# A GEGLU feed-forward kernel on one core: x's first tokens loaded in two halves of D, the first weight half tiles over ScalarE, and the products of the first two blocks side by side

## The chip, the core and the metric

The kernel runs on one core of a Trainium2 chip. The core has a matrix engine (TensorE, called PE in the profile, with its weight loads shown apart as PEld), three elementwise engines (VectorE = DVE, ScalarE = ACT, GpSimd = POOL) and SyncE (SP), which here issues nearly all DMAs. Each engine takes its instructions in program order. The engines run beside each other and wait for each other on semaphores. The metric is the device time of one execution in microseconds (us), lower is better.

## What is computed

```python
B, S, D, F = 32, 32, 1024, 3584          # all operands bf16
# x (B,S,D), w_gate (D,F), w_up (D,F), w_down (F,D)
def reference(x, w_gate, w_up, w_down):
    return (_gelu(x @ w_gate) * (x @ w_up)) @ w_down
```

There are 1024 tokens (B times S). Both stages are large matrix products: 1024 x 1024 x 7168 for gate and up, and 1024 x 3584 x 1024 for down.

## The kernel before

**Stage 1** (to about 184 us) computes gate and up for one block of 128 columns of F at a time, 28 blocks in all. It treats each block as a 2 by 2 block product and does it with seven products instead of eight (the Winograd form of Strassen). The rows of the left side are gate and up, and its columns are the two halves of D: `a11`, `a12` are the block's w_gate for the first and second half of D, `a21`, `a22` the same of w_up. The right side is x transposed: `B11`, `B21` hold the first 512 tokens for the first and second half of D, `B12`, `B22` the other 512 tokens. Each product is 4 matmuls of 128 x 128 by 128 x 512 (`KH` = 4 steps of 128 along half of D).

The products by their names in the code, for block i:

- first (P1) a11 x B11 and second (P2) a12 x B21 accumulate in the same PSUM tile `A[i]`, bf16 operands. P1 alone is copied out by ScalarE to `E1`, and after P2 ScalarE writes gelu(A) to `GL`. These two need only w_gate and the first tokens.
- fifth (P5) S1 x T1 into `Y[i]`; sixth (P6) S2 x T2 and seventh (P7) S3 x T3 accumulate in `X[i]`, which ScalarE has seeded with E1 (`seed`). After P6 ScalarE copies X out (`E2`), after P7 again (`e3`), and VectorE adds e3 and Y to `U1`. Fourth (P4) C22 x T4 goes on in X, third (P3) S4 x B22 goes on in Y.
- The sums S1 to S4 are made for each block from the four weight tiles, `C22` is a copy of a22; T1 to T4 are sums of the B tiles and are made once, by VectorE, after all of x has landed (`t_sum`, lines 245 to 248). All of these are fp32 for the PE.

In PSUM four buffers with tag "p" hold the warm-up results and then the X tiles, four with tag "q" hold the A and Y tiles. A new A or Y waits until the tile four places before it has been read.

**Order around the change.** The program order is written by hand. The time before the first data is filled by 18 warm-up matmuls on zeros (`NWARM`, line 136). SyncE issues, in this order: the transposing DMA of the first 512 tokens (1 MB, `xt0`, line 135), the second D half of gate tile 0 (two blocks of columns, 512 KB whole), gate tile 1, the first two blocks of up tile 0, gate tiles 2 and 3, the transposing DMA of the other 512 tokens (`xt1`, line 146), gate tile 4, the rest of up tile 0. The first D half of gate tile 0 is issued by ScalarE, after a small Copy that reads the result of warm-up matmul 3. While x's second half is on its way, PE does P1 and P2 of blocks 0 to 7 (`LEAD` = 8, lines 255 to 262; P2 of block 7 comes later). Then follow P5 of blocks 0 and 1, P1 of block 8 and P2 of block 7 (`ahead()`, line 279), P6 and P7 of blocks 0 and 1 one block after the other, P1 of 9 and P2 of 8, and P4 and P3 of both. VectorE in the same time makes the sums of blocks 0 and 1 (lines 241 to 244), T1 to T4, and the early sums of block 2; GpSimd starts on its sums when its instruction `held` (line 252) has seen the end of T4.

**The loop** (line 296) then goes over blocks 2 to 27. Each pass does P6 and P7 and P5 of block i, P4 and P3 of block i-1, and in most passes P1 and P2 of blocks further on. GpSimd makes most of the sums.

**Stage 2** (line 328 on) does the down projection in the same seven-product form from the tile `gT`. The change does not touch it.

Of the kernel before, what the change touches and what calls it, by code (L numbers as in the profile page):

```python
# [12 lines left out]
def kernel(  # L13
# [18 lines left out]
    nc = tc.nc  # L32
# [16 lines left out]
    assert N == 2 * NB and DT % 2 == 0 and D % DB == 0 and FT % 4 == 0  # L49
    NWARM = 18  # L50
    LEAD = 8
# [29 lines left out]
    def load_gate(c, queue, lo=0, hi=DT):  # L81
        if c not in WG:
            WG[c] = gw.tile([P, DT, 2 * P], bf16, name="gw", tag="gw")
        queue.dma_start(
            out=WG[c][:, lo:hi, :], in_=wg_r[:, lo:hi, 2 * c * P : (2 * c + 2) * P]
        )
# [12 lines left out]
    def a11(i):  # L99
        return block(WG, 2, i, 0)  # L100

    def a12(i):
        return block(WG, 2, i, 1)
# [21 lines left out]
    def psum_q(name):  # L125
        return psum.tile([P, NB], fp32, name=name, tag="q")

    with tc.manual_schedule():
# [5 lines left out]

        nc.sync.dma_start_transpose(out=xt0, in_=xf[0:NB, :])
        for n in range(NWARM):
            nc.tensor.matmul(warm[n % 4], lhsT=zt[:, 0:P], rhs=zt, start=True, stop=True)
            if n == 3:
                nc.scalar.activation(table, warm[n][:, 0:8], ACT.Copy)
                load_gate(0, nc.scalar, 0, KH)  # L140
        load_gate(0, nc.sync, KH, DT)
        load_gate(1, nc.sync)
        load_up(0, 0, 2)
        load_gate(2, nc.sync)
        load_gate(3, nc.sync)
# [35 lines left out]

        def first_product(i):
            A[i] = psum_q("a")
            product(A[i], a11(i), B11)
            if i % 2 == 0:
                E1[i // 2] = ring.tile([P, 2, NB], fp32, name="e1", tag="ring")
            nc.scalar.activation(E1[i // 2][:, i % 2, :], A[i], ACT.Copy)  # L187

        def second_product(i):
            product(A[i], a12(i), B21, first=False)  # L190
            if i % 2 == 0:
                GL[i // 2] = half.tile([P, 2, NB], bf16, name="gl0", tag="half")
            nc.scalar.activation(GL[i // 2][:, i % 2, :], A[i], ACT.Gelu_apprx_tanh)

# [5 lines left out]

        done = 0

        def ahead():
            nonlocal done
            if done < FT:
                first_product(done)
            if done:
                second_product(done - 1)
            done += 1

        def sixth_product(i):
            product(X[i], S2[i], T["T2"], first=False)
            E2[i] = epool.tile([P, NB], fp32, name="e2", tag="e2")
            nc.scalar.activation(E2[i], X[i], ACT.Copy)  # L214

# [7 lines left out]

        def seventh_product(i):
            product(X[i], S3[i], T["T3"], first=False)
            e3 = epool.tile([P, NB], fp32, name="e3", tag="e3")
            nc.scalar.activation(e3, X[i], ACT.Copy)  # L227
            U1[i] = epool.tile([P, NB], bf16, name="u1", tag="u1")
            nc.vector.tensor_tensor(U1[i], Y[i], e3, ALU.add)  # L229

# [38 lines left out]
        for k in range(KH):  # L269
            for i in range(2):  # L270
                nc.tensor.matmul(  # L271
                    Y[i],
                    lhsT=S1[i][:, k, :],
                    rhs=T["T1"][:, k, :],
                    start=(k == 0),
                    stop=(k == KH - 1),
                    skip_group_check=True,
                )
# [12 lines left out]
        copy_a22(2)  # L291
        finish(0)
# [3 lines left out]
        for i in range(2, FT + 1):  # L296
            here, prev, more = i < FT, i - 1 if i > 2 else None, i + 1 < FT
            if more:
                early_sums(i + 1)
            if here:  # L300
                sixth_product(i)
                if more:
                    seed(i + 1)
# [11 lines left out]
            if here:  # L315
                seventh_product(i)
                if more:
                    copy_a22(i + 1)
# [197 lines left out]
```

## Time and profile before

| | |
|---|---|
| time, median of 3 runs | 277.59 us (277.51 to 277.72) |
| the profiled execution's own time | 277.56 us |
| its span in the profile | 275.8 us (1.76 us lie outside) |
| PE busy | 270.0 us, 98% of the span |
| PEld / DVE / ACT / POOL busy | 190.5 / 189.2 / 138.1 / 88.6 us |
| moved by DMA | 26.42 MB, mean 96 GB/s |
| granted TensorE clock | 9 tenths or more in all 40 slices |

The page of the profile lists busy times, the span in 40 slices, DMA queues, the chain of work that ended last, groups of instructions, and DMA issues. In a line of a timeline the first number is the start in us from the span's start, the second how long it took in us, then engine, source line, operation, output and input by their names in the program, how many there are (x), and in brackets how long the engine sat idle before and what released it. "SPq" and "ACTq" are DMAs issued by SyncE and ScalarE; their data moves in the DMA queues q1 and q10. In a list of DMA issues the last number is the median time in us from issue to landing.

### The profile page before, as it was taken

What the parts mean: (1) busy time and instruction counts of PE and PEld (TensorE: products, weight loads), DVE (VectorE), ACT (ScalarE), POOL (GpSimd) and SP (SyncE); (2) the same over time, 40 slices, a digit from 0 to 9 for tenths busy, and PEclk for the clock granted to TensorE, in tenths of its full rate; (3) what the DMA queues carried; (4) which work ended last, traced back from release to release, by engine and by line L of the source; (5) the groups of instructions that cost most, each with busy time, mean ns of one, the idle gap of its engine ahead of it and who ended that gap; (6) DMA issues with size and microseconds to landing.
All of it is one profiled execution on the core that took longest, in us unless ns stands there. A gap on an engine that the chain in (4) does not pass through costs nothing.

```text
span 275.8 us, 3328 instructions
## 1 busy us (share of the span) xinstructions
PE 270.0 (98%) x1179; PEld 190.5 (69%) x1194; DVE 189.2 (69%) x227; ACT 138.1 (50%) x237; POOL 88.6 (32%) x81
## 2 busy tenths in 40 slices
PE   8999999999999999999999999999999999999995
PEld 3446767777677776777766777764447888888883
DVE  0279865667666676666766555759994999999900
ACT  2488475665656665666656666532100082870311
POOL 0000484458554585545854444600000000000000
PEclk9999999999999999999999999999999999999999
DMA  8996420522062071152420120259702000000221
GB/s 194 286 280 157 150 71 5 156 77 76 18 212 76 0 225 37 46 154 76 154 76 9 67 58 22 88 188 324 239 0 76 2 0 0 0 2 0 96 96 38
DMA packets 40912, 26.42 MB, mean 96 GB/s; under 512 B 9152, under 2 KB 40896, under 8 KB 40896
## 3 DMA queue, kind: packets, MB, share of 16 engines
q1 hardware_dynamic: 40224, 25.82, 32.0%
q10 hardware_dynamic: 672, 0.39, 0.5%
q8 instruction: 9, 0.15, 0.2%
q14 instruction: 7, 0.06, 0.1%
HBM read 22.02 MB, written 2.10 MB: 87 GB/s over the span
## 4 chain that ended last, share of the span: by engine, by line
PE 96%; DMA 3%; issue 0%; ACT 0%
PE x L113 28%; PE x L371 18%; PE y L113 18%; PE a L113 17%; PE y L371 9%; PE z L371 4%; DMA xt<-in_x_dram 3%; PE y L271 1%; ACT o_sb L483 0%
## 5 line engine op out<-in xcount | busy, mean ns | idle before, releaser
L113 PE MATMUL x<-T,s 128*128 128x512 f32 x224 | 63.5, 408 | 0.0
L113 PE MATMUL a<-xt,gw 128*128 128x512 bf16 x212 | 51.0, 380 | 1.1 <-DMA xt<-in_x_dram 0.4
L175 POOL TENSOR_TENSOR s<-gw,s 128x512 fp32r<-128x512 bf16 x26 | 30.4, 1171 | 62.4 <-PE y L113 61.7
L113 PEld LDWEIGHTS x<-T,s 128*128 128x128 f32 x224 | 41.7, 188 | 10.8 <-ACT e L214 0.4
L229 DVE TENSOR_TENSOR u<-y,e 128x512 bf16<-128x512 f32 x28 | 19.2, 690 | 34.8 <-ACT e L227 34.1
L171 DVE TENSOR_TENSOR s<-s,gw 128x512 fp32r<-128x512 f32 x28 | 40.8, 1457 | 0.0
L113 PEld LDWEIGHTS <-gw 128*128 128x128 bf16 x224 | 20.2, 98 | 27.6 <-issue 5.7
L218 DVE TENSOR_TENSOR gT<-gl,x 128x512 bf16<-128x512 bf16 x28 | 19.1, 686 | 18.4 <-PE x L113 18.4
L236 ACT ACTIVATE gl<-h 128x512 bf16<-128x512 bf16 x28 | 17.7, 631 | 27.4 <-DVE h L234 27.4
L113 PE MATMUL x<-T,c 128*128 128x512 f32 x112 | 30.2, 393 | 0.0
L113 PE MATMUL y<-B,s 128*128 128x512 f32 x112 | 30.0, 391 | 0.0
L167 POOL TENSOR_TENSOR s<-gw,uw 128x512 fp32r<-128x512 bf16 x25 | 29.2, 1168 | 0.0
L166 POOL TENSOR_TENSOR s<-uw 128x512 fp32r<-128x512 bf16 x25 | 29.1, 1164 | 0.0
L187 ACT ACTIVATE e<-a 128x512 f32<-128x512 f32 x28 | 16.7, 597 | 22.9 <-PE a L113 22.8
L113 PE MATMUL y<-T,s 128*128 128x512 f32 x104 | 27.8, 389 | 0.0
L371 PE MATMUL x<-tc,sc 128*128 128x512 f32 x112 | 25.7, 389 | 0.0
L113 PEld LDWEIGHTS y<-B,s 128*128 128x128 f32 x112 | 21.0, 188 | 4.8
L113 PEld LDWEIGHTS x<-T,c 128*128 128x128 f32 x112 | 20.9, 188 | 4.8 <-ACT e L227 0.5
L371 PEld LDWEIGHTS x<-tc,sc 128*128 128x128 f32 x112 | 21.0, 188 | 4.4
L227 ACT ACTIVATE e<-x 128x512 f32<-128x512 f32 x28 | 16.8, 599 | 14.4 <-PE x L113 14.4
L113 PEld LDWEIGHTS y<-T,s 128*128 128x128 f32 x104 | 19.5, 188 | 4.1
L371 PEld LDWEIGHTS <-gT 128*128 128x128 bf16 x112 | 10.9, 98 | 13.2 <-issue 0.3
(52 smaller groups left out, 325.0 us busy)
## 6 DMA issues: line engine op xcount, KB each, us to landing
gw<-in_w_gate_dram SPq DMA_DIRECT2D x13, 512.0 KB, 3.9
uw<-in_w_up_dram SPq DMA_DIRECT2D x6, 1024.0 KB, 6.4
v<-in_w_down_dram SPq DMA_DIRECT2D x5, 512.0 KB, 3.8
v<-in_w_down_dram SPq DMA_DIRECT2D x4, 640.0 KB, 7.9
v<-in_w_down_dram SPq DMA_DIRECT2D x8, 256.0 KB, 4.3
out_dram<-o_sb SPq DMA_DIRECT2D x15, 128.0 KB, 1.7
uw<-in_w_up_dram SPq DMA_DIRECT2D x2, 512.0 KB, 6.0
gw<-in_w_gate_dram ACTq DMA_DIRECT2D x1, 256.0 KB, 4.4
```

Of the source, the lines that this page charges most:

```text
L113: nc.tensor.matmul(ps, lhsT=lhs[:, k, :], rhs=rhs[:, k, :], start=(first and k == 0), stop=(k == KH - 1), skip_group_check=True,)
L166: engine.tensor_tensor(S1[i], a21(i), a22(i), ALU.add)
L167: engine.tensor_tensor(S3[i], a11(i), a21(i), ALU.subtract)
L171: nc.vector.tensor_tensor(S2[i], S1[i], a11(i), ALU.subtract)
L175: engine.tensor_tensor(S4[i], a12(i), S2[i], ALU.subtract)
L187: nc.scalar.activation(E1[i // 2][:, i % 2, :], A[i], ACT.Copy)
L218: nc.vector.tensor_tensor(gT[:, i, 0:NB], GL[i // 2][:, i % 2, :], X[i], ALU.mult)
L227: nc.scalar.activation(e3, X[i], ACT.Copy)
L229: nc.vector.tensor_tensor(U1[i], Y[i], e3, ALU.add)
L236: nc.scalar.activation(G1[i], h1, ACT.Gelu_apprx_tanh)
L271: nc.tensor.matmul(Y[i], lhsT=S1[i][:, k, :], rhs=T["T1"][:, k, :], start=(k == 0), stop=(k == KH - 1), skip_group_check=True,)
L371: nc.tensor.matmul(ps, lhsT=lhs[:, i, t * P : (t + 1) * P], rhs=rhs[:, i, :], start=(first and j == 0 and i == 0), stop=(last and j == JF ...
```

## The change

The transposing load of the first 512 tokens is cut in two: `B11` (first half of D) is loaded first. ScalarE then issues the first half of gate tile 0 after warm-up matmul 1 instead of 3, and writes 8 columns into `B21`; because of that write SyncE's load of `B21`, which overwrites them, waits for ScalarE. ScalarE also issues the second half of gate tile 0, after warm-up matmul 8 (before, SyncE issued it). Gate tile 1 comes in two DMAs, and the first blocks of up tile 0 come behind gate tile 2 instead of before it. There are 11 warm-up matmuls instead of 18.

In the stretch of the first blocks, P2 of block 7 is done before P5 of blocks 0 and 1, and the work on ScalarE between the blocks is reordered. P6 of blocks 0 and 1 are done side by side (two steps of one block, two of the other, and so on), and so are P7. P1 of blocks 8 and 9 lie between P5, P6 and P7, and P2 of block 8 behind P7. P4 and P3 go block by block. VectorE makes the early sums of block 2 after the `U1` of both blocks instead of before, `held` now reads S2 of block 2, and GpSimd makes S1 and S3 of block 3 before S4 of block 2. From block 3 on the loop is as before.

```diff
-    NWARM = 18
+    NWARM = 11
...
-        nc.sync.dma_start_transpose(out=xt0, in_=xf[0:NB, :])
+        nc.sync.dma_start_transpose(out=B11, in_=xf[0:NB, 0 : KH * P])
         for n in range(NWARM):
             nc.tensor.matmul(warm[n % 4], lhsT=zt[:, 0:P], rhs=zt, start=True, stop=True)
-            if n == 3:
-                nc.scalar.activation(table, warm[n][:, 0:8], ACT.Copy)
-                load_gate(0, nc.scalar, 0, KH)
-        load_gate(0, nc.sync, KH, DT)
-        load_gate(1, nc.sync)
+            if n in (1, 8):
+                nc.scalar.activation(table, warm[n % 4][:, 0:8], ACT.Copy)
+                load_gate(0, nc.scalar, *((0, KH) if n == 1 else (KH, DT)))
+            if n == 1:
+                nc.scalar.activation(B21[:, 0, 0:8], table, ACT.Copy)
+        nc.sync.dma_start_transpose(out=B21, in_=xf[0:NB, KH * P : D])
+        load_gate(1, nc.sync, 0, KH)
+        load_gate(1, nc.sync, KH, DT)
+        load_gate(2, nc.sync)
         load_up(0, 0, 2)
-        load_gate(2, nc.sync)
         load_gate(3, nc.sync)
         nc.sync.dma_start_transpose(out=xt1, in_=xf[NB:N, :])
         load_gate(4, nc.sync)
...
+        def pair_product(ps, lhs, rhs, first, cuts):
+            for lo, hi in zip(cuts, cuts[1:]):
+                for p, l in zip(ps, lhs):
+                    for k in range(lo, hi):
+                        nc.tensor.matmul(
+                            p,
+                            lhsT=l[:, k, :],
+                            rhs=rhs[:, k, :],
+                            start=(first and k == 0),
+                            stop=(k == KH - 1),
+                            skip_group_check=True,
+                        )
...
+        def sixth_products(*blocks):
+            cuts = range(0, KH + 1, 2)
+            pair_product([X[i] for i in blocks], [S2[i] for i in blocks], T["T2"], False, cuts)
+            for i in blocks:
+                E2[i] = epool.tile([P, NB], fp32, name="e2", tag="e2")
+                nc.scalar.activation(E2[i], X[i], ACT.Copy)
...
-        early_sums(2, nc.vector)
-        second_sum(2)
-        held = spool.tile([P, 8], f32r, name="held", tag="held", bufs=1)
-        nc.gpsimd.tensor_copy(held, T["T4"][:, KH - 1, 0:8])
-
-        between = {2: lambda: copy_a22(0), 4: lambda: seed(0), 6: lambda: seed(1)}
+        between = {2: lambda: seed(0), 4: lambda: seed(1), 6: lambda: copy_a22(0)}
         for n in range(0, LEAD, 2):
-            first_product(n)
-            first_product(n + 1)
+            first_products(n)
+            first_products(n + 1)
             if n in between:
                 between[n]()
-            second_product(n)
-            if n + 2 < LEAD:
-                second_product(n + 1)
-        done = LEAD
+            second_products(n)
+            second_products(n + 1)
...
-        ahead()
-        sixth_product(0)
-        sixth_product(1)
-        seventh_product(0)
-        seventh_product(1)
-        ahead()
+        first_products(8)
+        sixth_products(0, 1)
+        first_products(9)
+        seventh_products(0, 1)
+        second_products(8)
+        early_sums(2, nc.vector)
+        second_sum(2)
         seed(2)
-        fourth_product(0)
-        fourth_product(1)
-        third_product(0)
-        third_product(1)
+        held = spool.tile([P, 8], f32r, name="held", tag="held", bufs=1)
+        nc.gpsimd.tensor_copy(held, S2[2][:, KH - 1, 0:8])
+        early_sums(3)
         late_sums(2)
+        for i in range(2):
+            fourth_product(i)
+            third_product(i)
         copy_a22(2)
         finish(0)
...
         for i in range(2, FT + 1):
             here, prev, more = i < FT, i - 1 if i > 2 else None, i + 1 < FT
-            if more:
+            if more and i > 2:
                 early_sums(i + 1)
             if here:
-                sixth_product(i)
+                sixth_products(i)
```

`seventh_products` is cut the same way as `sixth_products`; `first_products` and `second_products` are the old functions for one or more blocks.

More of the change, by code (lines that the diff above doesn't have):

```diff
@@ L180, with first_products, second_products @@
         A, E1, GL = {}, {}, {}
[L182 to L193, printed above, removed]
+        def pair_product(ps, lhs, rhs, first, cuts):
[10 more added lines that the diff above has]
+                        )
+        def first_products(*blocks, cuts=(0, KH)):
+            for i in blocks:
+                A[i] = psum_q("a")
+            pair_product([A[i] for i in blocks], [a11(i) for i in blocks], B11, True, cuts)
+            for i in blocks:
+                if i % 2 == 0:
+                    E1[i // 2] = ring.tile([P, 2, NB], fp32, name="e1", tag="ring")
+                nc.scalar.activation(E1[i // 2][:, i % 2, :], A[i], ACT.Copy)
+        def second_products(*blocks, cuts=(0, KH)):
+            pair_product([A[i] for i in blocks], [a12(i) for i in blocks], B21, False, cuts)
+            for i in blocks:
+                if i % 2 == 0:
+                    GL[i // 2] = half.tile([P, 2, NB], bf16, name="gl0", tag="half")
+                nc.scalar.activation(GL[i // 2][:, i % 2, :], A[i], ACT.Gelu_apprx_tanh)
         X, Y, E2, U1, G1 = {}, {}, {}, {}, {}
@@ L199, in seed @@
             nc.scalar.activation(X[i], E1[i // 2][:, i % 2, :], ACT.Copy)
-        done = 0
+        done = LEAD + 2
         def ahead():
@@ L205, in ahead @@
             if done < FT:
-                first_product(done)
-            if done:
-                second_product(done - 1)
+                first_products(done)
+            second_products(done - 1)
             done += 1
[L211 to L214, printed above, removed]
+        def sixth_products(*blocks):
+            cuts = range(0, KH + 1, 2)
+            pair_product([X[i] for i in blocks], [S2[i] for i in blocks], T["T2"], False, cuts)
+            for i in blocks:
+                E2[i] = epool.tile([P, NB], fp32, name="e2", tag="e2")
+                nc.scalar.activation(E2[i], X[i], ACT.Copy)
         def fourth_product(i):
@@ L222, in fifth_product, with seventh_products @@
             product(Y[i], S1[i], T["T1"])
[L224 to L229, printed above, removed]
+        def seventh_products(*blocks):
+            cuts = range(0, KH + 1, 2)
+            pair_product([X[i] for i in blocks], [S3[i] for i in blocks], T["T3"], False, cuts)
+            for i in blocks:
+                e3 = epool.tile([P, NB], fp32, name="e3", tag="e3")
+                nc.scalar.activation(e3, X[i], ACT.Copy)
+                U1[i] = epool.tile([P, NB], bf16, name="u1", tag="u1")
+                nc.vector.tensor_tensor(U1[i], Y[i], e3, ALU.add)
         def third_product(i):
@@ L268 @@
             Y[i] = psum_q("y")
[L269 to L278, printed above, removed]
-        ahead()
-        sixth_product(0)
-        sixth_product(1)
-        seventh_product(0)
-        seventh_product(1)
-        ahead()
+        pair_product(
+            [Y[0], Y[1]], [S1[0], S1[1]], T["T1"], True, range(KH + 1)
+        )
+        first_products(8)
[5 more added lines that the diff above has]
+        second_sum(2)
         seed(2)
-        fourth_product(0)
-        fourth_product(1)
-        third_product(0)
-        third_product(1)
+        held = spool.tile([P, 8], f32r, name="held", tag="held", bufs=1)
+        nc.gpsimd.tensor_copy(held, S2[2][:, KH - 1, 0:8])
+        early_sums(3)
         late_sums(2)
+        for i in range(2):
+            fourth_product(i)
+            third_product(i)
         copy_a22(2)
@@ L315 @@
             if here:
-                seventh_product(i)
+                seventh_products(i)
                 if more:
```

## The prediction

> **What bounds the kernel now.** I read the chain that ended last first, because it tells whether any engine but PE matters; then its pieces in order of time, to find what is not PE; then the timeline of the first 35 us and the DMA queues in short windows, since the change lies there.
>
> ```profile
> PE 96%; DMA 3%; issue 0%; ACT 0%
> ...
> 0.73 7.18 DMA xt<-in_x_dram
> 7.91 0.04 issue
> 7.96 6.85 PE a L113 x31
> 14.81 0.05 issue
> 14.86 6.21 PE a L113 x28
> 21.07 1.85 PE y L271 x8
> 22.91 1.74 PE a L113 x8
> 24.65 3.75 PE x L113 x16
> ```
>
> The chain is 7.96 us of waiting for the first tokens and then PE without a break to 272.4 us. The change leaves PE's matmuls as they are, 7 warm-ups apart, so it can win time only by starting the row of products earlier, and lose it only by breaking the row. A matmul costs 13.11/60 = 0.2185 us here (7.96 to 21.07, 60 matmuls by the code). P1 of blocks 0 and 1 are 8 of them, 1.75 us, so P2 of block 0, the first to need the second half of D, starts at 9.71. That instant is the yardstick: behind it both kernels have the same PE work, and if no new gap opens the end moves as it moves.
>
> ```profile
> 1.19 6.33 PE L137 MATMUL warm<-zt 128*128 128x512 bf16 x18 [1.19 <-DVE zt L130]
> 3.17 0.18 ACT L139 ACTIVATE table<-warm 128x8 bf16<-128x8 f32 x1 [0.94 <-PE warm L137]
> 3.19 0.43 ACTq L84 DMA_DIRECT2D gw<-in_w_gate_dram  x1
> 4.59 1.11 SPq L84 DMA_DIRECT2D gw<-in_w_gate_dram  x2
> 7.67 0.10 PEld L113 LDWEIGHTS <-gw 128*128 128x128 bf16 x1 [0.65 <-DMA gw<-in_w_gate_dram]
> 19.26 2.50 DVE L157 TENSOR_TENSOR T<-xt,xt 128x512 fp32r<-128x512 bf16 x4 [1.86 <-DMA xt<-in_x_dram]
> 26.22 2.35 DVE L157 TENSOR_TENSOR T<-xt,T 128x1024 fp32r<-128x1024 bf16 x2
> 34.32 0.69 DVE L234 TENSOR_TENSOR h<-y,e 128x512 bf16<-128x512 f32 x1 [0.70 <-ACT gl L236]
> ```
>
> See here that the first weights come hardly before x (7.67 against 7.96), and that VectorE stands still until 19.26 for x's other tokens and is then busy to 34. The queues, in the windows 5.5 to 6 and 6 to 6.5 us:
>
> ```profile
> q1 hardware_dynamic: 523, 0.13, 117.7%
> q10 hardware_dynamic: 27, 0.01, 9.6%
> ...
> q10 hardware_dynamic: 290, 0.15, 106.5%
> q1 hardware_dynamic: 52, 0.01, 11.7%
> ```
>
> ScalarE's queue (q10) moved nothing before about 5.85, though its load was issued at 3.19: it waited until the transposing load on SyncE's queue (q1) was nearly through. Then it ran almost alone for 0.9 us. q1's next load began only at 6.7, though issued at 4.59. Summed in steps of 0.2 us, the transposing load moves from 2.1 to 6.15, has 2048 of its 4096 packets done at 4.2, and is seen landed at 7.91, 1.76 us behind its last data. A weight half tile is seen 0.7 us after its last data.
>
> **The change, part by part.** The sum is made against the profiled execution, 277.56 us, 0.03 under the median of the runs; I count these as equal.
>
> *First half of x alone.* B11 is half the packets: data to 4.2, seen between 4.65 (the other transposing load was seen about 0.45 behind its last data, 18.7 against 19.13) and 5.96 (1.76 behind). I take 5.96, the row of the same place.
>
> *Gate half tile over ScalarE.* Warm-up 1 ends two slow matmuls in; these stand 0.427 apart. 3.17 - 2 x 0.427 = 2.31, the issue at 2.33, its data behind B11 from 4.2 to 5.1, seen at 5.8. The warm-ups cost 11 x 0.427 and end at 5.9: the weight loads step at 0.43 until 5.43 and at 0.22 from 5.85, so what is dropped is the 7 fast ones. P1 thus starts near 6.0 and is through at 7.75.
>
> *The held half.* ScalarE's Copy into B21 comes after its DMA issue (0.43), at 2.76, and ends at 2.95; SyncE issues B21 at 3.0 instead of as part of the first load. The whole load's issue held SyncE 3.79 us, so a half 1.9, to 4.9. Behind it in SyncE's queue stand all weight loads and xt1. First data comes 1.3 to 1.4 us after an issue (0.73 to 2.1), so at 4.4, when the gate half tile still fills the engines: no hole. B11, B21 and the half tile have the same bytes as xt0 and the half tile before, whose data ended at 6.95. So B21's data ends at 6.95 and is seen between 7.4 (+0.45) and 8.7 (+1.76). I take 8.7: as before, another queue's load runs beside its end.
>
> *The second gate half tile.* Its issue waits for warm-up 8: 1.19 + 9 x 0.427 + 0.27 (the release in the line at 3.17) = 5.3, against 4.59 on SyncE before. Its landing is what the trace of before does not show. Lower bound: it does what ScalarE's load did before, starts at 6.6 or as B21's data ends, runs almost alone while q1 stands between two loads, and is seen at 6.95 + 0.9 + 0.7 = 8.55. Middle: it shares the engines with gate tile 1, issued by SyncE at 4.9 and 5.4; both half tiles end at 8.75, seen at 9.45. Upper bound: it waits behind the whole of gate tile 1, as long as that took from issue to landing (5.2), so 10.5. I take 8.7, nearest to the only row in which the two queues met behind a transposing load.
>
> The Trainium skill, "DMA: Bandwidth & Descriptors", section "Issuing engines are not separate DMA queues", says that DMAs of all issuing engines interleave on the same 16 engines, so another queue saves only issue time. By that rule the half tile shares with gate tile 1 and lands at 9.45. This trace disagrees for the first load (q10 idle from its issue to 5.85, then alone), so I hold the rule for the second case, not the first.
>
> So P2 of block 0 starts at 8.8 (B21 or gate, 8.7, and 0.05 to 0.1 to start) and not at 9.71: **0.9 us earlier**. PE stands from 7.75 to 8.8, so it does not matter whether P1 begins at 6.0 or 7.0.
>
> *What is late next.* up tile 0's first blocks come behind gate tile 2, 512 KB later at 290 GB/s: at 13.97, where gate tile 2 landed before, not at 12.24. VectorE's 8 sums (12.25 to 17.40, 5.15 us) then end at 19.1. Their cover is the wait for xt1 to 19.26: 0.14 us are left, cost 0. xt1 itself has the same bytes ahead of it. GpSimd has nothing yet.
>
> *P5 and the pairs.* All 64 matmuls of blocks 0 to 7 now end at 8.8 + 56 x 0.2185 = 21.05, so P5 starts when it did before, and the last piece of T1, ready at 21.75, is needed at 22.4. P1 of block 8 to 23.8, P6 from there (T2 whole at 24.03, its second half needed at 24.7), P1 of 9 to 26.5, P7 to 28.3 (T3 at 26.3; E2 of block 1 at 26.4, needed at 26.95), P2 of 8 to 29.2. P4 of block 0 needs T4 (28.57). Cost 0 to -0.1: the row of 16 matmuls took 3.75 us where the f32 rows of 4 at 0.91 give 3.64. I take 0.
>
> *VectorE after T4.* U1 of both blocks, 1.28, then three sums of block 2, 1.81, then gT, h1, gT, h1 at 0.64 to 0.69: 28.49 + 1.28 (or 29.9, by e3 of block 1) + 1.81 + 2.7 = 34.3 to 34.4 for the last h1. It frees the PSUM of block 1's Y, which P1 of block 10 needs; PE is there at 35.62 - 0.9 = 34.7. Slack 0.3; cost 0, and every us by which xt1 is later costs the rest. With no slack used, this wait caps the gain at about 1.3.
>
> *GpSimd's order.* `held` waits for S2 of block 2, at 31.7, and took 1.79; S1 of block 3 at 34.7, VectorE's S2 of block 3 by 36.4 (it took 1.64 beside GpSimd), needed by P6 of block 3 at 37.1. S4 of block 2 at 37.1 is needed near 43. Cost 0; its cover is the 0.7 us. ScalarE's cost in the blocks, about 3.0 of each 3.5 us, is unchanged.
>
> Sum: 277.56 - 0.9 = **276.66, say 276.7 us**.
>
> **The rivals.**
>
> *A tie by sharing.* The second half tile shares with gate tile 1 and is seen at 9.45; P2 starts at 9.5, gain 0.2, 277.35 (277.05 to 278.1 with small losses). For it: its issue is 0.7 us later than before, and gate tile 1 is ahead of it. It also covers the change not doing what it says: B11 no earlier than x's whole now (7.91) puts P2 at 9.66, no gain. Against it: q10's row above.
>
> *Slower by the late gate half.* The half tile's descriptors wait behind all of gate tile 1, as ScalarE's first load waited 2.66 us for its first packet. Then it is seen at 10.5, P2 starts at 10.55: +0.85, 278.4. It decides from 10.27 on (9.71 + 0.56). For it: a load of 256 KB took 4.4 us from ScalarE, and 5.32 + 5.2 = 10.5 is what the tile ahead takes. Against it: what held the first load was a transposing load of 1 MB; gate tile 1 is half that.
>
> *Slower by a slow PE.* The matmul rate doubled at 5.85, after 11 slow warm-ups, and now the warm-ups end right there, with a stand of 1 us soon behind. If PE is slow again from 8.8 for 16 matmuls, that is 16 x 0.21 = 3.35 us: 280.0; for 8, 278.3. Against it: the trace has 0.43 us idle at 7.5 with no slow matmul behind it, nothing longer. The Trainium skill, "TensorE: Matmul & The Clock Gate", Part 1, says that PE is slowed after an idle window of some 3.4 us, which a stand of 1 us is not; no run here shows it.
>
> *The gain eaten by VectorE.* xt1 0.5 us later takes 0.2 of the gain: 276.9; 1 us later 277.4. SyncE's split loads speak for it, the unchanged bytes against it.
>
> **How the numbers follow.** Under 0.2% of 277.59, 0.56 us, no measurement of this kernel tells a change from none: the bounds are 277.03 and 278.15. My forecast holds 0.50, with its own range 276.2 (gain 1.36, the cap and the small gap) to 277.0. The tie holds 0.23, VectorE 0.09 (two thirds of it still faster), the late gate half 0.12, the slow PE 0.06. Faster 0.50 + 0.06 = 0.56; same 0.23 + 0.03 = 0.26; slower 0.18. The range for 8 in 10 goes from 276.1 (0.1 below the cap, which is itself a sum of rows) through the tie to 278.4, the late gate half.
>
> **What would show it.** P1 starting near 6.0, and a stand of PE near 7.75 to 8.8 on DMA gw or DMA xt: how it ends decides between forecast, tie and late half. q10's packets between 6.6 and 8.8 show whether its load ran alone. x's other tokens at 19.3, PE without a break after 8.8, and no matmul of P1 at 0.43 apart show the rest. I am wrong if PE stands past 9.7, if T1 starts past 19.8, or if PE waits for VectorE near 34.

## The result and the profile after

The changed kernel takes 278.2 us (median of 10 runs, 277.81 to 278.43) against 277.56 us (277.45 to 277.72, 10 runs): a ratio of 1.0021, 95% interval 1.0012 to 1.0029. It is slower by 0.21%, where I had forecast 276.7 and a gain of 0.9 us. The profiled execution took 278.29 us with a span of 276.5.

The chain that ended last, of the changed kernel, in order of time (start, length, what):

```profile
1.19 1.84 PE warm L137 x4
3.03 7.08 DMA xt<-in_x_dram
10.11 0.14 issue
10.25 6.63 PE a L189 x30
...
22.50 1.84 PE y L189 x8
```

The same stretch in the timeline:

```profile
2.34 0.41 ACTq L84 DMA_DIRECT2D gw<-in_w_gate_dram  x1
3.03 3.75 SPq L143 DMA_TRANSPOSE xt<-in_x_dram  x1
...
6.93 1.90 PE L189 MATMUL a<-xt,gw 128*128 128x512 bf16 x8 [0.96 <-DMA gw<-in_w_gate_dram]
10.25 12.25 PE L189 MATMUL a<-xt,gw 128*128 128x512 bf16 x55 [1.41 <-DMA xt<-in_x_dram]
20.52 2.50 DVE L160 TENSOR_TENSOR T<-xt,xt 128x512 fp32r<-128x512 bf16 x4
```

P1 did start earlier (6.93 against 7.96), but PE then stood 1.41 us for the second half of x, and P2 of block 0 started at 10.25, not at 9.71 as before nor at 8.8 as forecast. Behind that instant PE does not break: P1 of block 10 starts at 36.16 (35.62 before) and the last ScalarE copy at 273.01 (272.46): 0.54 and 0.55 later, the 0.54 of P2. The rest of the 0.73 between the two profiled executions lies behind that copy.

What held B21 back is seen in the changed kernel's table by windows of half a microsecond. Its columns are the stretch and its length, the busy us of PE, PEld, DVE, ACT and POOL with the number of instructions, the granted clock, the mean busy share of the DMA engines, and GB/s:

```profile
4.50:5.00 0.50, 0.50 (x3) 0.15 (x2) 0.00 (x0) 0.00 (x0) 0.00 (x0) 1.00 0.89 250
5.00:5.50 0.50, 0.50 (x3) 0.15 (x1) 0.00 (x0) 0.18 (x1) 0.00 (x0) 1.00 1.08 257
5.50:6.00 0.50, 0.48 (x2) 0.00 (x0) 0.00 (x0) 0.00 (x0) 0.00 (x0) 1.00 2.39 127
6.00:6.50 0.50, 0.00 (x0) 0.00 (x0) 0.00 (x0) 0.00 (x0) 0.00 (x0) 1.00 0.41 53
6.50:7.00 0.50, 0.07 (x1) 0.07 (x2) 0.00 (x0) 0.00 (x0) 0.00 (x0) 1.00 0.80 170
7.00:7.50 0.50, 0.50 (x3) 0.24 (x4) 0.00 (x0) 0.00 (x0) 0.00 (x0) 1.00 1.28 291
```

B21's packets begin at 5.1, while ScalarE's gate half tile is still moving. From 5.5 to 6.5 the two together move 90 GB/s in the mean, where either alone moves 290. The share of 2.39 beside 127 GB/s says that packets were long under way in this stretch, not that there was much to move. Packet by packet in the trace, 17 transposing packets, normally 18 ns each, take 0.6 to 1.15 us, and all of them end together (6.71 to 6.74), 0.2 us after the last packet of the half tile (6.50). The hole costs 1.37 us: B21's last packet ends at 8.32, where the forecast had 6.95.

### The profile page after: what moved, and what is told of

The parts are those of the page before. It is cut to its first block, busy times and chain, and to the rows that moved or that the text cites. A ratio compares the mean times of both kernels' runs of the same rounds, so it can differ in the third digit from the quotient of the medians.

```text
span 276.5 us, 3323 instructions
## 1 busy us (share of the span) xinstructions
PE 268.6 (97%) x1172; PEld 189.8 (69%) x1187; DVE 189.1 (68%) x227; ACT 138.3 (50%) x239; POOL 87.0 (31%) x81
## 4 chain that ended last, share of the span: by engine, by line
PE 90%; DMA 6%; SPq 1%; ACT 1%; DVE 1%; issue 1%; ACTq 0%
PE x L189 19%; PE y L113 17%; PE a L189 17%; PE x L382 14%; PE y L382 9%; PE x L113 9%; PE z L382 4%; DMA v<-in_w_down_dram 4%; DMA xt<-in_x_dram 3%; SPq L353 1%; PE y L189 1%; PE warm L137 1%; DVE u L251 0%; ACT gl L258 0%; ACT e L249 0%
## 5 line engine op out<-in xcount | busy, mean ns | idle before, releaser
L189 PEld LDWEIGHTS x<-T,s 128*128 128x128 f32 x224 | 41.9, 188 | 10.6
L249 ACT ACTIVATE e<-x 128x512 f32<-128x512 f32 x28 | 16.7, 599 | 14.5 <-PE x L189 14.5
L212 ACT ACTIVATE gl<-a 128x512 bf16<-128x512 f32 x28 | 16.7, 596 | 8.1 <-PE a L189 7.7
```

The source lines that it names most:

```text
L189: nc.tensor.matmul(p, lhsT=l[:, k, :], rhs=rhs[:, k, :], start=(first and k == 0), stop=(k == KH - 1), skip_group_check=True,)
```

## The experiments

Theory F: a transposing load and a plain weight load that meet in the DMA engines at its start hold each other up. (The first expectations call this theory A.) Theory B: a second transposing load is slow by itself, so the cut is what costs. Theory C: part of the loss lies in the new order of the products. Theory E: ScalarE's issue at 5.3 sets off the stall. Theory G, for one run: the two kinds of load simply share the engines' time. In the table, times from profiled executions are in us; "ratio" is against the kernel before on the same chip, with its 95% interval.

| run | P1 starts | P2 starts | T1 starts | median | ratio |
|---|---|---|---|---|---|
| before | 7.96 | 9.71 | 19.26 | 277.56 | 1 |
| the change | 6.93 | 10.25 | 20.52 | 278.2 | 1.0021 (1.0012 to 1.0029) |
| order_only | 7.94 | 9.69 | 19.31 | 277.43 | 0.9999 (0.999 to 1.0008) |
| head_only | 6.93 | 10.5 | 20.52 | 278.56 | 1.0035 (1.0022 to 1.0048) |
| no_hold | 11.15 | - | 22.77 | 281.5 | 1.0115 (1.0075 to 1.0154) |
| lo_on_sp | 6.35 | 9.66 | 19.94 | 277.91 | 1.0015 (1.0006 to 1.0024) |
| hi_on_sp | 6.89 | 10.44 | 21.76 | 278.78 | 1.0042 (1.0028 to 1.0056) |
| all_sp | 6.19 | 9.66 | 20.79 | 278.83 | 1.0051 (1.0024 to 1.0078) |
| hold_long | 6.75 | 11.05 | 23.40 | 280.62 | 1.0102 (1.0086 to 1.0117) |
| four_first | 6.56 | 11.15 | 21.36 | 278.92 | 1.0042 (1.0027 to 1.0057) |
| act_early | 7.91 | 9.66 | 20.04 | 277.51 | 0.9995 (0.9985 to 1.0004) |
| lo_first | 5.98 | 9.70 | 20.53 | 277.83 | 1.0013 (1.0004 to 1.0023) |
| gate_first | 7.34 | 9.39 | 20.66 | 278.7 | 1.0045 (1.003 to 1.006) |
| split_x | 10.42 | - | 21.88 | 281.83 | 1.0146 (1.0129 to 1.0164) |
| split_late | 9.51 | 11.26 | 20.14 | 279.18 | 1.0068 (1.0042 to 1.0093) |
| lo_then_whole | 7.80 | 9.55 | 20.15 | 277.9 | 1.0003 (0.9994 to 1.0012) |

(P2 is read where PE stands before it; where PE does not stand, it is P1 and 1.75 us. For head_only it is counted back from P5: 21.86 less 52 matmuls of 0.2185; PE does not stand there, because it does P1 at half rate, 8 matmuls from 6.93 to 10.32. In four_first 16 matmuls lie before P2, so 11.15 is like 9.40 in the other rows.)

What PE waits for before P2 is not the same in all of them. In the change, lo_on_sp, hold_long and gate_first x's second half comes last. In hi_on_sp, all_sp, four_first and lo_first it is seen at 8.1 to 9.4, and PE waits for the second gate half tile, which is seen 1.4 to 1.7 us after it. A line of lo_first's timeline:

```profile
9.70 2.55 PE L186 MATMUL a<-xt,gw 128*128 128x512 bf16 x11 [1.39 <-DMA gw<-in_w_gate_dram]
```

### Is it the loads or the order?

order_only has the loads and the 18 warm-ups of the kernel before, and the products of the changed one:

```diff
-    NWARM = 11
+    NWARM = 18
-        nc.sync.dma_start_transpose(out=B11, in_=xf[0:NB, 0 : KH * P])
+        nc.sync.dma_start_transpose(out=xt0, in_=xf[0:NB, :])
...
```

> The loads and warm-ups of the kernel before, with the products, sums and ScalarE work in the order of the changed kernel. Theory A (the loss is made at the head: B21's load meets ScalarE's gate half tile in flight, both crawl, and P2 of block 0 starts at 10.25 instead of 9.71): the order costs nothing, P2 starts at 9.7, 277.5 us, within 0.2 of the kernel before. Theory C (part of the 0.6 us is lost by the new order, where pairs, `held` or VectorE make PE wait): 277.7 to 277.9, with a gap of PE between 20 and 45 us.

head_only is its counterpart, an edit of the kernel before:

```diff
-    NWARM = 18
+    NWARM = 11
-        nc.sync.dma_start_transpose(out=xt0, in_=xf[0:NB, :])
+        nc.sync.dma_start_transpose(out=B11, in_=xf[0:NB, 0 : KH * P])
...
+        nc.sync.dma_start_transpose(out=B21, in_=xf[0:NB, KH * P : D])
+        load_gate(1, nc.sync, 0, KH)
+        load_gate(1, nc.sync, KH, DT)
+        load_gate(2, nc.sync)
         load_up(0, 0, 2)
```

> The loads and 11 warm-ups of the changed kernel, with the order of products and sums of the kernel before. Theory A: P2 of block 0 starts at 10.25 again and the loss is all here, 278.1 to 278.3; and because T1 starts near 20.5 where the old order asks for it at 21.6 minus its place, a further 0 to 0.5 us may be lost behind it, which the new order hides. Theory C: 277.9 to 278.0, less than the whole change loses.

The order costs nothing (0.9999) and the loads lose all of it and more (1.0035): theory C falls. Not all of the "more" is the loads' or the order's: in head_only's profiled execution PE did P1 at half rate, 0.42 us a matmul, after a stand of only 0.87 us, and P2 is worth 10.5 there instead of 10.25. With the loads this late the new order is even of use: between P2 and the last copy head_only loses a further 0.2 us, since P2 is 0.8 later than before and its last copy (273.45) 0.99; the whole change loses nothing there. The side-by-side products cost what the prediction gave them, zero, where the head is the old one. A line of order_only's timeline for PE:

```profile
7.94 13.97 PE L186 MATMUL a<-xt,gw 128*128 128x512 bf16 x63 [0.64 <-DMA xt<-in_x_dram]
```

PE waits 0.64 us for x and then goes through P1 and P2 of eight blocks without standing.

### What does the held write do, and does the half tile's queue matter?

no_hold:

```diff
-            if n == 1:
-                nc.scalar.activation(B21[:, 0, 0:8], table, ACT.Copy)
```

> The changed kernel without ScalarE's write into B21, so SyncE issues B21's load right behind B11's, near 2.15 instead of 3.03. Theory A: q1 has no pause into which ScalarE's half tile could slip, it waits for both transposing loads as in the kernel before, no hole between 5 and 6.6; gate seen near 7.6, B21 near 7.9, P1 from 7.6 to 8.0, P2 at 9.4 to 9.7: 277.2 to 277.5. If the half tile still starts near 4.2, between the two loads, the crawl comes again and P2 is past 10: 278.2. Theory B (a second transposing load on the queue is slow by itself, whatever moves beside it): the hole stays, with nothing of q10 in it, B21 seen past 9.5, 278 or more.

lo_on_sp:

```diff
         nc.sync.dma_start_transpose(out=B11, in_=xf[0:NB, 0 : KH * P])
+        load_gate(0, nc.sync, 0, KH)
...
-            if n in (1, 8):
+            if n == 8:
...
-            if n == 1:
-                nc.scalar.activation(B21[:, 0, 0:8], table, ACT.Copy)
```

> The changed kernel with the first gate half tile issued by SyncE between B11 and B21, and no held write: one queue, so no plain load of the other queue is in flight when B21's load begins. Theory A: no hole; B11 to 4.3, half tile to 5.9, B21 to 7.7, seen 8.4 to 9.4; P1 near 6.7, P2 at 9.0 to 9.6: 276.9 to 277.5. Theory B: B21's load shows the hole again (its 2048 packets take over 3 us instead of 1.8), P2 past 10.2, 278.2 or more.

Without the held write the half tile meets B21 in mid-flow (its first packet comes at 4.7), where theory A had it wait as in the kernel before. From 5.4 to 6.4 the two move 3 to 13 packets in each 0.2 us, where a transposing load alone moves 226; P1 starts at 11.15, and the time is 1.15% worse than before, in part because PE then did eight matmuls at half rate (last section). So the write is no detail: it keeps most of the meeting away. With the half tile on SyncE's own queue the hole shrinks to 0.4 us (5.7 to 6.1; theory A had none), P2 is at 9.66, as early as before, and the last copy at 272.48 (272.46 before). That profiled execution took 277.73 us and is one of the better ones of its kernel: its runs go from 277.59 to 278.27, where the kernel before stays within 277.32 to 277.80 in the same session. Something differs from one execution to the next; whether it is the hole, one traced execution can't show.

### Is it ScalarE's second issue, or the meeting?

hi_on_sp takes the issue at 5.3 away, all_sp takes all early loads off ScalarE's queue, and hold_long lets B21's load start only when the half tile has landed:

```diff
 # hi_on_sp
-            if n in (1, 8):
+            if n == 1:
                 nc.scalar.activation(table, warm[n % 4][:, 0:8], ACT.Copy)
-                load_gate(0, nc.scalar, *((0, KH) if n == 1 else (KH, DT)))
+                load_gate(0, nc.scalar, 0, KH)
...
         nc.sync.dma_start_transpose(out=B21, in_=xf[0:NB, KH * P : D])
+        load_gate(0, nc.sync, KH, DT)
```

```diff
 # all_sp
         nc.sync.dma_start_transpose(out=B11, in_=xf[0:NB, 0 : KH * P])
+        load_gate(0, nc.sync, 0, KH)
...
-            if n in (1, 8):
-                nc.scalar.activation(table, warm[n % 4][:, 0:8], ACT.Copy)
-                load_gate(0, nc.scalar, *((0, KH) if n == 1 else (KH, DT)))
-            if n == 1:
-                nc.scalar.activation(B21[:, 0, 0:8], table, ACT.Copy)
         nc.sync.dma_start_transpose(out=B21, in_=xf[0:NB, KH * P : D])
+        load_gate(0, nc.sync, KH, DT)
```

```diff
 # hold_long
-            if n in (1, 8):
+            if n == 1:
                 nc.scalar.activation(table, warm[n % 4][:, 0:8], ACT.Copy)
-                load_gate(0, nc.scalar, *((0, KH) if n == 1 else (KH, DT)))
+                load_gate(0, nc.scalar, 0, KH)
+                load_gate(0, nc.scalar, KH, DT)
             if n == 1:
-                nc.scalar.activation(B21[:, 0, 0:8], table, ACT.Copy)
+                nc.scalar.activation(B21[:, 0, 0:8], WG[0][:, 0, 0:8], ACT.Copy)
```

> The changed kernel with the second gate half tile issued by SyncE behind B21, so ScalarE issues nothing at 5.3; its first half tile and the held write stay. Theory A (the gate half tile in flight on ScalarE's queue and B21's starting load make each other crawl): the hole from 5.6 to 6.6 stays, gate seen near 6.9, B21 near 10, the second half tile behind it: P2 at 10.3 to 10.6, 278.2 to 278.5. Theory E (the stall follows ScalarE's issue at 5.3 by 0.3 us; without it there is none): q1 runs on, B21's data end near 7.2, P2 at 9.2 to 9.6, 277.0 to 277.4.

> All early loads on SyncE's queue, in the order B11, first gate half tile, B21, second gate half tile, gate tile 1; no held write, nothing on ScalarE's queue. Theory A: like the run with the half tile between B11 and B21, only the short hole of some 0.4 us at B21's start may remain, second half tile seen near 9.5: P2 at 9.4 to 9.9, 277.2 to 277.8. Theory E: that short hole goes too, since nothing is issued beside B21: P2 at 9.0 to 9.4, 276.8 to 277.2.

> The changed kernel with both gate half tiles issued by ScalarE after warm-up 1, and the held write reading the landed first half tile, so that B21's load is issued only when that half tile is there. Theory A: the two loads no longer meet; the half tiles move alone at full rate from 4.2 (0.9 us each), the first is seen near 5.8, P1 starts near 6.0, and B21, issued near 6, moves from 7.3 at full rate with no hole and is seen near 10.5 because of the long hold: P2 near 10.6, 278.4. Theory B (a second transposing load is slow by itself): B21's 2048 packets take 3 us from 7.3, seen past 11.5, 279.4 or more. A first half tile seen no earlier than 6.8 would go against A.

In hi_on_sp the hole is there unchanged (5.8 to 6.6) though ScalarE issues nothing near it: theory E falls. What ScalarE's second load does cost is the landing: with it B21 is seen 1.8 us after its last packet (8.3 and 10.1 in the change), without it 0.55 (8.28 and 8.83 in hi_on_sp, where theory A had 10). That wins nothing here, since PE then waits for the second gate half tile, seen at 10.39. In all_sp the short hole of lo_on_sp stays (5.6 to 6.0), again with nothing on ScalarE's queue beside it. In hold_long B21 moves alone, and well. Its table by windows:

```profile
8.50:9.00 0.50, 0.15 (x1) 0.00 (x0) 0.00 (x0) 0.32 (x1) 0.00 (x0) 1.00 0.95 219
9.00:9.50 0.50, 0.00 (x0) 0.00 (x0) 0.00 (x0) 0.28 (x1) 0.00 (x0) 1.00 1.26 288
9.50:10.00 0.50, 0.00 (x0) 0.00 (x0) 0.00 (x0) 0.00 (x0) 0.00 (x0) 1.00 1.28 291
```

No packet stands, 288 to 291 GB/s from 9.0 on, seen landed 0.5 us behind its last data (10.4 and 10.9). So a second transposing load is not slow in itself when it starts on idle engines. Two expectations failed, though. The time is 280.62 and not 278.4, because P2 started at 11.05 instead of 10.6 and PE then did eight matmuls at half rate (last section). And the gate half tile was seen at 6.72 and not at 5.8. It is late with no transposing load beside it, as earlier windows of the same kernel show:

```profile
4.50:5.00 0.50, 0.50 (x3) 0.06 (x1) 0.00 (x0) 0.00 (x0) 0.00 (x0) 1.00 0.86 169
5.00:5.50 0.50, 0.05 (x1) 0.00 (x0) 0.00 (x0) 0.00 (x0) 0.00 (x0) 1.00 0.98 289
```

A plain load that starts as a transposing load has just ended runs at 169 GB/s for its first half microsecond, with a few of its packets taking 0.3 to 0.75 us instead of 27 ns. In the kernel before, the same half tile began a little before the end of x's load and ran at full rate at once.

four_first, on top of all_sp, issues the first halves of gate tiles 0 and 1 ahead of B21 and gives PE twice the work before it needs B21:

```diff
         load_gate(0, nc.sync, 0, KH)
+        load_gate(1, nc.sync, 0, KH)
         nc.sync.dma_start_transpose(out=B21, in_=xf[0:NB, KH * P : D])
...
+        for group in ((0, 1, 2, 3), (4, 5), (6, 7)):
+            for i in group:
+                first_products(i)
+            between[group[0]]()
+            for i in group:
+                second_products(i)
```

> All early loads on SyncE's queue, B11, then the first halves of gate tiles 0 and 1, then B21 and the second halves; P1 of blocks 0 to 3 come before any P2, so PE has 3.5 us of work instead of 1.75 while B21 is on its way. If the stand of PE before P2 is the whole loss and xt1 is not later than in the changed kernel: P1 from 6.0 to 6.5, P2 of block 0 near 10.3, which with 16 matmuls done is like 8.6 in the old count: 276.5 to 277.0. If the pauses of the one queue make xt1 later than 20.5, VectorE's sums take it back: 277.2 to 277.7, with PE waiting for T1 or for VectorE between 21 and 36.

PE stands less (P2 as if at 9.40), and the time is still 278.92. T1 starts at 21.36 and PE waits 0.43 us for it at P5. This was the case named last in the expectation; its time was 1.2 us above the figure there.

### The meeting at the other end, and less of it

act_early has the loads of order_only, but the half tile is issued at once and so meets x's whole load at its start:

```diff
+        load_gate(0, nc.scalar, 0, KH)
         nc.scalar.activation(table, zt[:, 0:8], ACT.Gelu_apprx_tanh)
...
-            if n == 3:
-                nc.scalar.activation(table, warm[n][:, 0:8], ACT.Copy)
-                load_gate(0, nc.scalar, 0, KH)
```

> The loads of the kernel before with the products in the new order, one thing changed: ScalarE issues the first gate half tile at once, near 0.73, beside SyncE's issue of the whole transposing load, so that a plain load is in flight when the transposing one begins. Theory F (a transposing load moves in step on all 16 engines, and stands until the last engine has done with a plain load that came before it): x, landed at 7.9 before, is seen later than 8.2, with a hole of q1 between 2.5 and 4.5 and single packets of 0.3 us or more; 277.8 or more. Theory G (plain and transposing loads simply share the engines' time): the same bytes arrive at the same time, x seen at 7.3 to 7.9, 277.0 to 277.5.

lo_first and gate_first are all_sp with the first half of gate tile 0, or the whole tile, issued ahead of B11:

```diff
 # lo_first
+        load_gate(0, nc.sync, 0, KH)
         nc.sync.dma_start_transpose(out=B11, in_=xf[0:NB, 0 : KH * P])
-        load_gate(0, nc.sync, 0, KH)
```

```diff
 # gate_first
+        load_gate(0, nc.sync)
         nc.sync.dma_start_transpose(out=B11, in_=xf[0:NB, 0 : KH * P])
-        load_gate(0, nc.sync, 0, KH)
         nc.sync.dma_start_transpose(out=B21, in_=xf[0:NB, KH * P : D])
-        load_gate(0, nc.sync, KH, DT)
```

> All early loads on SyncE's queue: the first gate half tile before B11, then B11 and B21 with nothing between, then the second half tile and gate tile 1. Theory F: no plain load stands before B21, so B21 follows B11 without the hole of the changed kernel; B11 seen near 5.9, P1 from 6.0, B21's data end near 7.2; the second half tile starts after a pause of 0.6 and is seen at 9.2 to 9.6: P2 near 9.4, 277.2, between 276.9 and 277.5. Theory B (a second transposing load is slow by itself): hole at B21's start all the same, P2 past 10, 278 or more.

> All early loads on SyncE's queue: the whole of gate tile 0 first, then B11 and B21, then gate tile 1. Only one meeting of a plain load with a starting transposing load, at B11, near 3.9. Theory F: B11 waits for the slowest engine of gate tile 0, some 0.3 us, is seen near 6.6; B21 follows without a hole, data end near 7.7, seen 0.7 later as in the run with the long hold: P1 from 6.7, P2 at 8.5 to 8.9, 276.4 to 276.9, if gate tile 1 is there by 10.2. Theory B: B21 stands at its start and is seen past 10, 278 or more.

In act_early the meeting is there: q1 and q10 together move 205 GB/s from 2.6 to 3.8, transposing packets stand up to 0.56 us and all end together near 4.0, and x's data end at 7.4 instead of 6.15. Yet x is seen at 7.86, as before: it is now seen 0.5 behind its data, where before, with ScalarE's load moving beside its end, it took 1.76. The two cancel; neither theory had that (F had x past 8.2, G 277.0 to 277.5 with x at 7.3 to 7.9). lo_first puts P2 where it was, with T1 1.3 us later. gate_first has the earliest P2 of all, 9.39 (theory F had 8.5 to 8.9), and loses nevertheless. Its chain in order of time:

```profile
4.52 4.82 DMA xt<-in_x_dram
...
9.39 12.26 PE a L185 x56
21.65 2.29 PE y L185 x8
...
37.51 1.88 PE x L185 x8
39.39 1.19 PE x L113 x4
```

P5 takes 2.29 us instead of 1.85, since the last piece of T1 comes late, and P4 of block 2 takes 1.19 instead of 0.96 (in order_only). The weight load before that P4 waits for ScalarE's e3, which stands in ScalarE's order behind the two gelu that wait for VectorE's last h1 (34.87, against 34.32 before). Its line in the timeline:

```profile
39.38 0.77 PEld L113 LDWEIGHTS x<-T,c 128*128 128x128 f32 x4 [0.42 <-ACT e L245]
```

This is the fourth rival of the prediction, the gain eaten by VectorE: T1 at 20.66 is 1.4 us late, and takes back 0.32 us of gain and 0.44 more (last copy 272.90 against 272.46). The profiled execution is one of the two fastest of its eight (278.07 to 279.89); what the slower ones lose beyond that, no trace shows.

T1 is late because of one more meeting. xt1 starts behind a plain load on its own queue. In before, the change, order_only, head_only and lo_on_sp that load's last packet ends within 0.06 us of xt1's first; no packet stands, and xt1's data take 3.7 us. In the other eleven runs the plain load's packets go on for 0.5 to 1.9 us beside xt1, 11 to 23 transposing packets stand (the longest 0.5 to 1.7 us) until 0.4 us after the plain load's last packet, and xt1's data take 4.1 to 5.5 us. In gate_first this is 0.8 of the 1.4 us, in all_sp 1.3 of its 1.5.

### The cut alone, with and without a meeting

split_x is order_only with nothing changed but the cut; split_late differs from it only in when ScalarE issues the half tile:

```diff
 # split_x
-        nc.sync.dma_start_transpose(out=xt0, in_=xf[0:NB, :])
+        nc.sync.dma_start_transpose(out=B11, in_=xf[0:NB, 0 : KH * P])
+        nc.sync.dma_start_transpose(out=B21, in_=xf[0:NB, KH * P : D])
 # split_late, on top of it
-            if n == 3:
+            if n == 8:
```

> The loads and 18 warm-ups of the kernel before with the products in the new order, and one thing changed: the first transposing load is cut in two, B11 and B21 issued one right behind the other; ScalarE issues the first gate half tile after warm-up 3, near 3.19, as before. Theory F with its second part (a plain load gets between only at a seam between two transposing loads; ready near 4.5, it misses the seam at 4.2): B21 runs on behind B11 without a hole, the half tile waits to near 6 and is seen near 7.6, P1 starts at 7.7 since B11 is there long before, P2 at 9.4: 277.1 to 277.5. If the half tile still gets in between the two, single packets stand 0.3 us or more, q1 has a hole between 4.5 and 6, P2 starts past 10 and the time is 278.2 or more. Theory B (a second transposing load is slow by itself): a hole of q1 with nothing of q10 in it.

> The kernel of the run before this one (the loads of the kernel before with x's first load cut in two) with one change: ScalarE issues the first gate half tile after warm-up 8 instead of 3, at 5.3 instead of 3.2, so its data can't come before 6.5. Theory F (only the plain load beside B21 makes the hole): q1 runs at full rate through both halves to 6.2 with no packet of 0.25 us or more, the half tile follows and is seen near 8.2, P1 near 8.3, P2 near 10.0: 277.7 to 278.0. Theory B (the cut itself makes it): q1 falls under half its rate between 4.5 and 6.5 though nothing of q10 moves, x's last packets come past 7, P2 past 10.5: 278.4 or more.

The tables by windows, first of split_x:

```profile
5.00:5.50 0.50, 0.50 (x5) 0.21 (x3) 0.00 (x0) 0.00 (x0) 0.00 (x0) 1.00 1.58 209
5.50:6.00 0.50, 0.50 (x4) 0.26 (x3) 0.00 (x0) 0.00 (x0) 0.00 (x0) 1.00 1.46 63
6.00:6.50 0.50, 0.50 (x4) 0.21 (x3) 0.00 (x0) 0.00 (x0) 0.00 (x0) 1.00 0.86 83
```

and of split_late:

```profile
4.50:5.00 0.50, 0.50 (x2) 0.15 (x1) 0.00 (x0) 0.00 (x0) 0.00 (x0) 1.00 1.23 251
5.00:5.50 0.50, 0.50 (x3) 0.22 (x2) 0.00 (x0) 0.18 (x1) 0.00 (x0) 1.00 1.27 288
5.50:6.00 0.50, 0.50 (x3) 0.22 (x2) 0.00 (x0) 0.00 (x0) 0.00 (x0) 1.00 1.28 290
6.00:6.50 0.50, 0.50 (x4) 0.17 (x3) 0.00 (x0) 0.00 (x0) 0.00 (x0) 1.00 0.67 148
6.50:7.00 0.50, 0.50 (x4) 0.23 (x3) 0.00 (x0) 0.00 (x0) 0.00 (x0) 1.00 0.57 61
```

This pair settles the main point. With the half tile issued at 3.2 it gets in beside B21 (in 6.0 to 6.5 q10 has 30 packets and q1 102), and x's last packets come at 8.8 instead of 6.15. Issued at 5.3, it stays out, and both halves of x run through to 6.4, at 251 to 290 GB/s up to 6.0, 0.2 us later than the whole load of before; x is even seen a us earlier than before, at 6.9. So here the cut cost nearly nothing, and the meeting cost over 2 us. I had expected the half tile to stay out in split_x too, since in the kernel before it did: beside the whole load, issued at the same 3.19, it waited for the end. That part of the theory fell. split_late is slow all the same for the other reason: behind x's end the plain loads start at 61 GB/s (6.5 to 7.0), the half tile on q10 moves only from 7.5 to 8.9, and P1 starts at 9.51, not 8.3.

The Trainium skill, "DMA: Bandwidth & Descriptors", section "Issuing engines are not separate DMA queues", says that DMAs of different issuing engines interleave on the same 16 engines. In split_x they do, but at 63 to 83 GB/s together from 5.5 to 6.5, where either kind reaches 290 alone.

lo_then_whole is order_only with the half tile on SyncE's queue ahead of x's whole load:

```diff
+        load_gate(0, nc.sync, 0, KH)
         nc.sync.dma_start_transpose(out=xt0, in_=xf[0:NB, :])
...
-                load_gate(0, nc.scalar, 0, KH)
```

> The loads of the kernel before with the products in the new order, 18 warm-ups, x's first load whole, and the first gate half tile issued by SyncE ahead of it instead of by ScalarE. Theory F: the half tile moves alone from 1.8 to near 2.9, x's load starts behind it with a short stand, data end near 7.0, seen 0.7 later since no other queue moves beside its end: P1 at 7.7, P2 at 9.45, 277.2 to 277.4. If x is seen 1.7 behind its data as in the kernel before, P1 starts at 8.7 and the time is 278.2.

P1 and P2 start 0.16 us earlier than before, T1 0.9 later, and the time is the same (1.0003). No version here beats the kernel before.

### What stays open

In lo_first and gate_first x's second half moved slowly with no plain load near it: 158 to 217 GB/s from 5.0 to 6.5 in lo_first, 72 GB/s from 6.5 to 7.0 in gate_first. So the seam between two transposing loads on one queue cost from 0.2 us (split_late) to about 1 us (gate_first, where B21's packets took from 5.9 to 8.8 and not the 2.0 us of the second half in the kernel before). Theory B is therefore not dead in this weak form, and why the seam is cheap in one kernel and dear in another wasn't found. Nor was it found why plain loads start slowly behind a transposing load, why the plain load ahead of xt1 ends cleanly in some kernels and not in others, or why the half tile waits beside the whole load of before and gets in beside B21 in split_x.

## Why the prediction was wrong

The yardstick held: P2's start was forecast to carry the end, and moved it by 0.55 for 0.54.

The step that failed is in the part on the held half: "First data comes 1.3 to 1.4 us after an issue (0.73 to 2.1), so at 4.4, when the gate half tile still fills the engines: no hole." The two loads did overlap, and the overlap is what made the hole. I summed bytes, at one rate for any mix; but the trace of before shows no transposing load that starts beside another queue's plain one (the one that starts right behind a plain load of its own queue, xt1 at 15.04, has no hole), so that rate had no row, and I should have put an unknown with two ends there. What I read as a waiting queue (q10 silent to 5.85) had a second meaning: before, the two kinds had been kept apart but for 0.3 us at the end. B21's data began at 5.1 instead of 4.4 and ended at 8.32 instead of 6.95, and 1.37 of the 1.45 us by which P2 missed its forecast (10.25 against 8.8) are this term. The landing behind the data took 1.8 us; I had 1.76.

The measured 278.2 lies inside my range (276.1 to 278.4), and that is luck: the upper end came from the late gate half, which did not happen, and the load that did come late had no price among my rivals.

The other steps, in their order:

- B11 was seen at 4.9 (0.74 and 4.2 from issue to landing), near the lower end of my two, not the 5.96 that I took. It mattered for nothing, since the gate half tile came after it.
- The first gate half tile was seen at 6.9, not 5.8. As the prediction said, P1 anywhere up to 7.0 costs nothing by itself; but the slow half tile is also what B21 ran into. hold_long shows that 0.9 of this 1.1 is there without a transposing load beside it.
- SyncE's issue of B21 took 3.75 us and not 1.9 (B11's took 1.41). Everything behind it on SyncE moved, xt1's issue from 10.13 to 11.27. But that is not what made T1 late (20.52, not 19.26): from B21's end to xt1's first packet the loads ran on at 288 GB/s, so xt1's data started 1.25 us later (16.29, not 15.04) because of the hole. The prediction's "the same bytes ahead of it" was right and not enough.
- The second gate half tile behaved as in my lower bound: q10 ran alone as B21's data ended (8.2 to 8.8), and it was seen 4.5 after its issue, at 9.8. It was late because B21 was, and none of the three bounds on it decided. But it came only 0.3 us before x's second half, and x's half early is not enough by itself: in all_sp and lo_first that was seen at 8.1 and 8.2, and PE waited for this tile until 9.7. Both rivals on this tile (the tie and the late half) picked the wrong load; "x's other D half late" was no rival of mine, though it was among the things that were to show me wrong.
- P6 and P7 side by side, the moved P1 and P2, `held` and GpSimd's order: 0, as costed. `held` took 0.19 us here, not the 1.79 of before.
- A slow PE: in the profiled execution stands of 0.96 and 1.41 us left the rate alone (the first 8 matmuls of P1 took 1.90, full rate). The rival was alive all the same: head_only has the same loads and warm-ups, and its P1 ran at half rate, 3.4 us, of which the wait for x hid all but some 0.25.
- VectorE as the next bound was right in kind. It did not decide in the changed kernel, whose P2 was later than T1 needed; it decided in gate_first and four_first, and in all_sp, hi_on_sp and lo_first too P5 or P4 of block 2 took longer than in order_only.

## What to carry to other kernels

Cutting a load to start earlier is paid for where the pieces meet other loads: before counting bytes at one rate, look for a row where the two kinds of load move at the same time, and treat the pair as unknown if there is none. A DMA queue that is silent behind another may be doing its neighbour a service. When PE never waits in the profile, an earlier start is worth only as much as the next arrival allows; here x's other tokens and VectorE's chain took back what gate_first won.

## What the runs showed of the hardware that I had not expected

A transposing load seems to move in step on all 16 DMA engines: when it stands, some 7 to 23 packets stand together (18 ns become 0.3 to 1.7 us), and they are released at one instant. For x's first tokens that instant is 0.2 us after the last packet of the plain load ahead in seven runs (the change, head_only, hi_on_sp, lo_on_sp, all_sp, four_first, act_early), whichever queue that load is on. For xt1 it is 0.4 us after it in eleven. In split_x, no_hold and gate_first packets also stand in several groups, which this does not explain.

A transposing load is seen about 0.5 us after its last data in most cases (hold_long, act_early, split_late), and 1.7 to 1.8 us after it in before, the change, order_only, head_only, lo_on_sp and split_x, where ScalarE's load moves beside its end. In before its closing 4-byte packets move only at 6.8 to 6.9, with those of ScalarE's load; in hi_on_sp they move at 8.0 to 8.3, with the last data. The condition is not complete: B11 of the change was seen 0.5 us after its data with ScalarE's load just starting, and B11 of gate_first 1.4 us after with no other queue moving.

PE's rate can halve after fewer idle microseconds than I had allowed for. In hold_long it stood 1.69 us, worked for 1.9, stood 2.41, and the next 8 matmuls took 3.39 us, 0.42 each (mean granted clock 0.55 from 11.0 to 14.5). A line of its timeline:

```profile
11.05 3.39 PE L190 MATMUL a<-xt,gw 128*128 128x512 bf16 x8 [2.41 <-DMA xt<-in_x_dram]
```

After stands of 3.48 us (split_x) and 5.92 us (no_hold) the same is seen, and part of what these three lose is this. The Trainium skill, "TensorE: Matmul & The Clock Gate", Part 1, speaks of an idle window of some 3.4 us; here 2.41 us, with 1.69 us shortly before, were enough.

head_only shows the other side. All 11 of its warm-up matmuls ran at 0.43 us, and after 0.87 us of idle so did the 8 of P1, with a granted clock of 1.00 in the profile. In the changed kernel the warm-ups were as slow, and P1 after 0.96 us of idle was fast. So 11 warm-ups were not enough in every execution.
